# Routing table of a mixture-of-experts kernel: indirect scatters to DRAM replaced by one-hot products

## Chip, cores and metric

The kernel runs on one core of a Trainium2 chip. The metric is the device time of the core in microseconds (us). The kernel before was timed in three runs: 739.37 us in the median, 734.49 to 740.71.

## The reference, cut to what matters

Two blocks follow each other. The first is attention over 8 batches, 8 heads, 576 positions and a head width of 64, half of the heads with a local mask of 32 positions, half with a strided one. Its output, 512 columns for each of the 4608 positions, is the input x of the second block, a mixture of 8 experts. Each position goes to exactly one expert, and which one depends on the positions ahead of it in its batch:

```
for s in range(S):
    fresh_e = int(np.argmax(logits[b, s]))
    if s == 0 or local_gate[b, s] < 0.5:
        e = fresh_e
    else:
        e = prev_e if prev_e >= 0 else fresh_e
    prev_e = e
    ...
    h = np.maximum(x[b, s] @ w1[e], 0.0)
    out[b, s] = p[e] * (h @ w2[e])
```

w1[e] is 512 x 1024 and w2[e] is 1024 x 512; p is the softmax of the logits. All is fp32.

## The kernel before

**Attention.** The loop of attention() (L414-L445) goes over 32 steps n, one for each of 8 batches and 4 pairs of heads, and three more to drain. It is a software pipeline written out by hand: at step n the scores of n (L252, exp on ScalarE at L256, mask on VectorE at L263), the values of n-1 (L276, norm at L289-L290), the transposes of n-2 (L317), the gate logits of a batch (L336) and its gates (L354-L379). Stores of x to DRAM (L301, L307) and all loads go out from SyncE's queue. Other work is hung on steps by two lists: `also[n]`, and `steps`, the 16 VectorE sums and differences of the first expert's weights that a Strassen-like product needs (L703: first four tiles ws1-ws4 of w1, two ops each, then wt1-wt4 of w2). Two of these are issued at each step from n=9 on.

**Routing** is done in two rounds of four batches. Router.steps (L511-L570) gives for each position a slot (idx) and a gate value (p): transposes (L523), scans on VectorE (L529, L536), products for the counts (L541, L542) and back (L556). A slot says place within the 128 rows of a tile (lane), tile and expert. Round 0 hangs on steps 19 to 23 of attention, round 1 on the first pair of the experts' part.

**The table** tells which token and gate value stands in which slot, 128 lanes x 56 columns (NT). It lies in DRAM (slots). It is filled with "no token" at the start (L503-L505). Each round then scatters its (token, gate) pairs to it with 20 indirect DMAs of GpSimd (L577), one for each of 5 chunks of 128 positions and 4 batches, each with up to 128 entries of 8 bytes. At the end it is read back once (fetch, L643) and turned to gather indices (table, L647). Round 0's scatters hang on steps m=24 to 33, two a step, and share GpSimd's queue with the gathers of x (L737). Since the experts start before round 1 is done, the first four tiles (columns of experts 0 and 1, two tiles each) are also made on chip from round 0 alone (early, L585-L639): for each of 20 groups of positions a one-hot matrix of lanes (L620) and a matrix `put` of 20 columns, a one-hot of 4 columns times five bf16 values (L615), are multiplied on TensorE and summed over the 20 groups (L627). The five values are exact parts: the token number as 64 a + b, the gate as three bf16 pieces.

**Experts.** Each expert gets its weights by SyncE's queue into one of two buffers W[0], W[1]. Two tiles of 128 rows make a pair: pair_hidden (seven products L807, VectorE adds L795, ScalarE copies L814 and relus L794) and pair_output (L843, L854-L857), with gather (L737), scale (L743), transposes (L750), row sums (L759) and a scatter of the result (L763) around them. A list of places is run at fixed points in between: four in pair_hidden, four in pair_output; it holds the round's steps, the weight sums of the next expert and the scatters (L1002-L1020). The first pair is expert 0's, the second, `other`, expert 1's, the third, `second`, again expert 0's, with rows of round 1. A count of tiles per expert then picks an arm of a switch (L975); arms() (L649) makes it.

[...] GpSimd's queue holds scatters, gathers and, later, output scatters one behind the other.

Of the kernel before, what the change touches and what calls it, by code (L numbers as in the profile page):

```python
# [93 lines left out]
@with_exitstack  # L94
def attention_then_scomoe(ctx: ExitStack, tc: tile.TileContext, qkl, qks, vl, vs, wg, q, k, vl2, vs2, wg2, w1, w2, out):
    nc = tc.nc
    dram = ctx.enter_context(tc.tile_pool(name="dram", bufs=1, space=DRAM))
    xd = dram.tile([N, D], F32, name="xd")
    keep = ctx.enter_context(tc.tile_pool(name="keep", bufs=1))
    ident = keep.tile([P, P], F32, name="ident")  # L100
    make_identity(nc, ident)

    with ExitStack() as fast:
        once = fast.enter_context(tc.tile_pool(name="once", bufs=1))
        router = Router(once, dram, tc, ident)
        one = Weights(once)
        spot = (once.tile([P, 2, D], F32, name="x0"), once.tile([P, 2, DK, P], F32, name="xt"),
                once.tile([P, 4, 2, P], F32, name="tt"))
        with tc.manual_schedule():
            moe = Experts(nc, tc, xd, w1, w2, out, ident, router, one, spot)  # L110
            with ExitStack() as part:
                attention(part, tc, qkl, qks, vl, vs, wg, xd, ident, router, moe)
            with ExitStack() as part:
                moe.run(part)
        flag = router.flag


    redo = nc.values_load(flag, min_val=0, max_val=P + N,
                          skip_runtime_bounds_check_because="a count of at most 128 rows and of pairs")
    with tc.If(redo > 0):  # L120
        with ExitStack() as slow:
            general(slow, tc, q, k, vl2, vs2, wg2, w1, w2, xd, out, ident)
# [20 lines left out]
def attention(ctx, tc, qkl, qks, vl, vs, wg, xd, ident, router, moe):  # L143
# [260 lines left out]
    also[n] += [lambda: early.extend(router.early(bank, moe.spot)), lambda: early.pop(0)()]  # L404
    for n in range(m + 1, m + 6):
        also[n].append(lambda: early.pop(0)())
    for i, do in enumerate(router.scatters(0)):
        also[m + i // 2].append(do)
# [5 lines left out]
    for n in range(len(units) + 3):  # L414
# [20 lines left out]
        for do in steps[:2] if n >= 9 else []:  # L435
            do()
            steps.remove(do)
# [10 lines left out]
class Router:  # L448


    def __init__(self, pool, dram, tc, ident):
# [6 lines left out]
        self.tok = f("tok", [P, CH, B, 2], I32)  # L458
# [9 lines left out]
        self.io, self.jc = f("io", [P, P], BF16), f("jc", [P, 2, EARLY])  # L468
        self.vals = f("vals", [P, CH, RB, 5], BF16)
        self.put = f("put", [P, CH * RB, 5, 2 * EARLY], BF16)  # L470
        self.pool = pool
        self.T = dram.tile([P * NT, 2], I32, name="slots")

    def constants(self):
# [19 lines left out]
        ids = pool.tile([P, CH, B], I32, name="ids")  # L494
        nc.gpsimd.iota(ids, pattern=[[P, CH], [S, B]], base=0, channel_multiplier=1)
        nc.vector.tensor_copy(self.tok[:, :, :, 0], ids)
        for name, pattern, mult, o in (("io", [[1, P]], 0, self.io), ("jc", [[E, 2], [1, EARLY]], 0, self.jc),
                                       ("v0", [[P // 64, CH], [S // 64, RB]], 0, self.vals[:, :, :, 0]),
                                       ("v1", [[0, CH], [0, RB]], 1, self.vals[:, :, :, 1])):
            t = pool.tile(list(o.shape), I32, name=f"i{name}")  # L500
            nc.gpsimd.iota(t, pattern=pattern, base=1 if name == "v0" else 0, channel_multiplier=mult)
            nc.vector.tensor_copy(o, t)
        nc.gpsimd.iota(self.tab[:, :, 0], pattern=[[0, NT]], base=SKIP, channel_multiplier=0)  # L503
        nc.gpsimd.iota(self.tab[:, :, 1], pattern=[[0, NT]], base=0, channel_multiplier=0)
        nc.gpsimd.dma_start(out=self.rows(0, XT, E), in_=self.tab.rearrange("p (k e) v -> p k e v", e=E))  # L505

    def rows(self, k0, k1, e):

        return self.T.rearrange("(k p e) v -> p k e v", p=P, e=E)[:, k0:k1, 0:e]

    def steps(self, r, bank):  # L511
# [39 lines left out]
        def back():  # L551
# [16 lines left out]
            nc.vector.tensor_copy(self.tok.bitcast(F32)[:, :, bs, 1], p)  # L568
# [3 lines left out]
    def scatters(self, r):  # L572
        def one(t, b):
            m = min(P, S - t * P)

            def do():
                s = self.nc.gpsimd.indirect_dma_start(  # L577
                    out=self.T, out_offset=bass.IndirectOffsetOnAxis(ap=self.idx[0:m, t, b:b + 1], axis=0),
                    in_=self.tok[0:m, t, r * RB + b], in_offset=None, bounds_check=P * NT - 1, oob_is_err=False)
                self.tc.declare_no_dep(s.ins, group="slots", reason="scatters write different slots")  # L580
                self.tc.add_to_no_dep_group("slots", s.ins)
            return do
        return [one(t, b) for b in range(RB) for t in range(CH)]

    def early(self, bank, spot):  # L585
# [4 lines left out]
        lo, hi, code, lof = f("elo", [P, n], I32), f("ehi", [P, n], I32), f("ecode", [P, n]), f("elof", [P, n])  # L590
        at, rest, got = f("at", [P, n, 2 * EARLY], BF16), f("rest", [P, CH, RB]), f("got", [P, 5, 2 * EARLY])
        num, skip, gs = f("num", [P, 2 * EARLY]), f("skip", [P, 2 * EARLY]), f("gs", [P, 2 * EARLY])
        idx, val = flat(self.idx), self.vals.rearrange("p t b v -> p (t b) v")

        room = (spot[1].rearrange("p a k x -> p (a k x)").bitcast(BF16), spot[2].rearrange("p i a x -> p (i a x)").bitcast(BF16))
        lane = lambda i: room[2 * i // n][:, i % (n // 2) * P:(i % (n // 2) + 1) * P]

        def where():
# [6 lines left out]
            nc.vector.tensor_tensor(at, across(self.jc.rearrange("p k e -> p (k e)"), [P, n, 2 * EARLY]),  # L605
                                    spread(code, [P, n, 2 * EARLY]), op=Alu.is_equal)

        def what():
            v = [self.vals[:, :, :, i] for i in range(5)]
            nc.vector.tensor_copy(v[2], self.p)  # L610
            nc.vector.tensor_tensor(rest, self.p, v[2], op=Alu.subtract)
            nc.vector.tensor_copy(v[3], rest)
            nc.vector.tensor_tensor(v[4], rest, v[3], op=Alu.subtract)
            for i in range(5):
                nc.vector.tensor_tensor(self.put[:, :, i], at, spread(val[:, :, i], [P, n, 2 * EARLY]), op=Alu.mult)  # L615

        def lanes(a, b):
            def do():
                for i in range(a, b):
                    nc.vector.tensor_scalar(lane(i), self.io, lof[:, i:i + 1], None, Alu.is_equal)  # L620
            return do

        def products():
            o = bank()[:, 0:10 * EARLY].rearrange("p (v j) -> p v j", v=5)
            for i in range(n):
                m = min(P, S - i // RB * P)
                nc.tensor.matmul(o, lhsT=lane(i)[0:m], rhs=self.put[0:m, i], start=(i == 0), stop=(i == n - 1))  # L627
            nc.vector.tensor_copy(got, o)

        def numbers():  # L630
            tab = self.tab1.rearrange("p k e v -> p (k e) v")
            nc.vector.scalar_tensor_tensor(num, got[:, 0], 64.0, got[:, 1], Alu.mult, Alu.add)
            nc.vector.tensor_tensor(gs, got[:, 2], got[:, 3], op=Alu.add)
            nc.vector.tensor_scalar(skip, num, 0.0, SKIP + 64.0, Alu.is_equal, Alu.mult)
            nc.vector.tensor_scalar(self.gi1.rearrange("p k e -> p (k e)"), num, -64.0, 0.0, Alu.add, Alu.max)
            nc.vector.tensor_tensor(tab.bitcast(F32)[:, :, 1], gs, got[:, 4], op=Alu.add)
            nc.vector.scalar_tensor_tensor(tab[:, :, 0], num, -64.0, skip, Alu.add, Alu.add)

        return [where, what, lanes(0, n // 2), lanes(n // 2, n), products, numbers]  # L639

    def fetch(self):

        self.nc.gpsimd.dma_start(out=self.tab.rearrange("p (k e) v -> p k e v", e=E), in_=self.rows(0, XT, E))  # L643

    def table(self):

        self.nc.vector.tensor_scalar(self.gi, self.tab[:, :, 0], N - 1.0, None, Alu.min)  # L647
# [79 lines left out]
class Experts:  # L727
# [41 lines left out]
    def run(self, ctx):  # L769
# [234 lines left out]
        self.gather(other)  # L1004
        todo = router.steps(1, bank)
        places = slots(todo, [2, 2, 1, 1]) + slots(sums, [2, 2, 2, 1, 1])
        more = router.scatters(1)
        for place, n in zip(places[4:], (4, 2, 2, 2, 2)):
            place += [more.pop(0) for _ in range(n)]
        output(self.first, W[0], pair_hidden(self.first, W[0], places), other, places)  # L1010
        second = rows(0, 1, (2, 3))
        places = slots(sums, [2, 2, 2, 2])
        for place in places:
            place += [more.pop(0) for _ in range(2)]
        arms = router.arms(bank)
        places[3].append(lambda: next(arms))
        places += [[lambda: next(arms), router.table, lambda: self.gather(second)]]
        h = pair_hidden(other, W[1], places)
        router.fetch()
# [484 lines left out]
```

## Time and profile before

| | before |
|---|---|
| median of 3 runs | 739.37 us |
| time of the profiled execution | 738.92 us |
| its span, first to last instruction | 737.2 us |
| granted TensorE clock, mean | 0.959 |
| TensorE matmul busy | 683.0 us, 93% |
| VectorE busy | 353.4 us, 48% |
| ScalarE busy | 195.5 us, 27% |
| GpSimd busy | 134.7 us, 18% |
| scatters of slots L577 | 40, 40.9 us of GpSimd |
| gathers of x L737 | 40, 40.4 us of GpSimd |
| scatters of results L763 | 40, 45.5 us of GpSimd |
| early table's products L627 | 20, 173 ns each in the trace with latency |
| attention, about | 0 to 199.6 us |
| experts | 199.6 us to the end |

PE is TensorE's matmul, PEld its weight load, DVE VectorE, ACT ScalarE, POOL GpSimd. The page cuts the span in 40 slices of 18.43 us; a digit is the busy share of a slice in tenths, and PEclk is the clock that TensorE was granted, in tenths. In a row of groups come line, engine, operation, output and inputs, count, busy time, mean of one, the idle time just before, and what ended it. In the timeline a row has start, length, engine, line, operation, count, and in brackets the idle time before it with what ended it: "issue" is a wait for nothing that the profile shows, "remote" a wait for an event of which it has no record.

### The profile page before, as it was taken

The page shows a single profiled execution, that of the slowest core. Times are in us where ns is not written, and L with a number is a line of the kernel's source. Part 1 is how long each engine was busy: PE and PEld are TensorE (multiplying, and loading weights), DVE is VectorE, ACT ScalarE, POOL GpSimd, SP SyncE. Part 2 cuts the span into 40 slices and gives each one's busy share as a digit, 9 for nine tenths or more (in the row PEclk, how much of TensorE's full clock was granted, in tenths as well). Part 3 has the DMA queues.
Part 4 walks back from the last instruction along what each step waited for, and adds up shares of the span by engine and source line. Part 5 has one row for each costly group of instructions (what it writes and reads, how often), then busy time and mean ns, then how long its engine had stood idle before and what let it go on. Part 6 is the DMA issues. An engine that isn't in the chain of part 4 may idle for free.

```text
span 737.2 us, 14832 instructions
## 1 busy us (share of the span) xinstructions
PE 683.0 (93%) x6034; PEld 586.5 (80%) x6034; DVE 353.4 (48%) x843; ACT 195.5 (27%) x357; POOL 134.7 (18%) x150
## 2 busy tenths in 40 slices
PE   7999999497899699999999999999999999999992
PEld 5878887385698589985998899999589899789961
DVE  6568766272466534451463265455126646524300
ACT  2544443141321122212222123122322222222210
POOL 3000001405127330221121120221012012111010
PEclk9999999597699899999999999999999999999997
DMA  9797887731360022615321711720171262010010
GB/s 325 275 328 267 279 286 256 249 84 52 95 228 30 3 86 67 238 38 173 109 74 47 254 47 50 251 73 21 39 257 59 76 210 66 32 37 30 18 50 13
DMA packets 37803, 95.33 MB, mean 129 GB/s; under 512 B 5230, under 2 KB 14446, under 8 KB 37632
## 3 DMA queue, kind: packets, MB, share of 16 engines
q1 hardware_dynamic: 29616, 73.77, 29.0%
q0 software_dynamic: 7488, 19.56, 8.4%
q8 instruction: 66, 1.08, 0.6%
q14 instruction: 105, 0.86, 0.4%
q10 hardware_dynamic: 528, 0.07, 0.1%
HBM read 74.41 MB, written 19.49 MB: 127 GB/s over the span
## 4 chain that ended last, share of the span: by engine, by line
PE 79%; issue 7%; DVE 5%; DMA 3%; another core or an unknown queue 3%; ACT 1%; POOL 1%; SPq 0%; DVEq 0%; POOLq 0%; ACTq 0%
PE mps L843 26%; PE lps L807 25%; PE vps L276 5%; PE sps L252 4%; PE tps L317 3%; PE lps L898 3%; PE mps L909 3%; PE xps L750 2%; DMA w1t<-in_w_dram 2%; PE mps L935 2%; PE lps L919 1%; PE sps L246 1%; PE tps L336 1%; PE vps L354 1%
## 5 line engine op out<-in xcount | busy, mean ns | idle before, releaser
L763 POOL DMA_INDIRECT out_dram<-y,tab x40 | 45.5, 1138 | 323.9 <-DVE y L795 217.4
L807 PE MATMUL lps<-tt,ws 128*128 128x128 f32 x768 | 91.5, 275 | 0.4 <-issue 0.2
L807 PEld LDWEIGHTS lps<-tt,ws 128*128 128x128 f32 x768 | 88.5, 192 | 0.8 <-DVE u L795 0.4
L843 PE MATMUL mps<-wt,k 128*128 128x256 f32 x384 | 85.6, 379 | 0.0
L843 PEld LDWEIGHTS mps<-wt,k 128*128 128x128 f32 x384 | 72.9, 190 | 9.9
L577 POOL DMA_INDIRECT slots<-tok,idx x40 | 40.9, 1023 | 147.5 <-DVE tok L568 135.9
L807 PE MATMUL lps<-xt,w1t 128*128 128x128 f32 x512 | 64.8, 281 | 2.6 <-ACT y L941 1.4
L807 PEld LDWEIGHTS lps<-xt,w1t 128*128 128x128 f32 x512 | 62.1, 196 | 6.1 <-ACT y L941 2.8
L795 DVE TENSOR_TENSOR h<-lps,u 128x512 f32<-128x512 f32 x48 | 33.2, 691 | 66.5 <-PE lps L807 57.3
L843 PE MATMUL mps<-w2t,h 128*128 128x256 f32 x256 | 61.3, 383 | 0.0
L737 POOL DMA_INDIRECT x<-xd,gi x40 | 40.4, 1009 | 112.5 <-PE lps L807 34.9
L252 PE MATMUL sps<-qk 64*128 64x96 f32 (+2 forms) x704 | 55.4, 288 | 4.9 <-issue 4.1
L252 PEld LDWEIGHTS sps<-qk 64*128 64x128 f32 (+2 forms) x704 | 45.5, 188 | 14.8 <-issue 12.5
L256 ACT ACTIVATE e<-sps 128x576 f32<-128x576 f32 (+1 forms) x64 | 41.2, 651 | 58.4 <-PE sps L252 40.8
L843 PEld LDWEIGHTS mps<-w2t,h 128*128 128x128 f32 x256 | 48.1, 193 | 6.0
L794 ACT ACTIVATE h<-h 128x512 f32<-128x512 f32 x48 | 30.3, 630 | 75.5 <-DVE h L795 71.7
L794 ACT ACTIVATE h<-lps 128x512 f32<-128x512 f32 x28 | 16.5, 594 | 86.8 <-PE lps L807 58.8
L795 DVE TENSOR_TENSOR u<-lps,p 128x512 f32<-128x512 f32 x16 | 11.1, 692 | 57.9 <-PE lps L807 32.3
L807 PE MATMUL lps<-xt,ws 128*128 128x128 f32 x256 | 33.1, 285 | 6.0 <-DVE h L795 6.0
L743 ACT ACTIVATE x<-x,tab 128x512 f32<-128x512 f32 (+1 forms) x40 | 27.2, 718 | 40.6 <-DMA x<-xd,gi 26.9
L807 PEld LDWEIGHTS lps<-xt,ws 128*128 128x128 f32 x256 | 31.5, 201 | 6.2 <-DVE h L795 6.2
L276 PE MATMUL vps<-vl,e 128*64 128x65 f32 x768 | 29.4, 235 | 7.0 <-issue 4.7
(222 smaller groups left out, 977.4 us busy)
## 6 DMA issues: line engine op xcount, KB each, us to landing
w1t<-in_w_dram SPq DMA_DIRECT2D x8, 2048.0 KB
w2t<-in_w_dram SPq DMA_DIRECT2D x8, 2048.0 KB
qk<-in_qkl_dram SPq DMA_DIRECT2D x16, 592.0 KB
qk<-in_qks_dram SPq DMA_DIRECT2D x16, 576.0 KB
vl<-in_vf_dram SPq DMA_DIRECT2D x8, 780.0 KB
vs<-in_vg_dram SPq DMA_DIRECT2D x8, 639.8 KB
xd<-xl SPq DMA_DIRECT2D x16, 288.0 KB
xd<-xs SPq DMA_DIRECT2D x64, 63.0 KB
```

The lines of the kernel that those rows point to most:

```text
L252: nc.tensor.matmul(ps[0:m, h, c:c + w], lhsT=t[r, S + j * width:S + j * width + m], rhs=t[r, j * width:j * width + w], start=(u.local and ...
L256: nc.scalar.activation(e[0:kb, :, 0:n], ps[0:kb, :, 0:n], Act.Exp, bias=0.0, scale=1.0 / DH ** 0.5)
L276: nc.tensor.matmul(ps[a * HALF:(a + 1) * HALF, h, i], lhsT=u.e[0:m, h, q0:q0 + HALF], rhs=vt[0:m, j, 2 * i2 + h], start=(i == 0 and h == 0 ...
L317: nc.tensor.transpose(ps[:, t], src[:, t], ident)
L577: s = self.nc.gpsimd.indirect_dma_start(out=self.T, out_offset=bass.IndirectOffsetOnAxis(ap=self.idx[0:m, t, b:b + 1], axis=0), in_=self.t ...
L737: self.nc.gpsimd.indirect_dma_start(out=r.x[0:r.m, i], out_offset=None, in_=self.xd[0:r.rows], in_offset=bass.IndirectOffsetOnAxis(ap=r.gi ...
L743: self.nc.scalar.activation(r.x[0:r.m, i], r.x[0:r.m, i], Act.Copy, scale=r.gate[i][0:r.m])
L763: s = self.nc.gpsimd.indirect_dma_start(out=self.out, out_offset=bass.IndirectOffsetOnAxis(ap=r.si[i][0:r.m], axis=0), in_=y[0:r.m, i], in ...
L794: relu = lambda o, i: nc.scalar.activation(o, i, Act.Relu)
L795: add = lambda o, i, p: nc.vector.tensor_tensor(o, p, i, op=Alu.add)
L807: nc.tensor.matmul(ps[:, f], lhsT=m[:, kk, f * P:(f + 1) * P], rhs=v[:, kk], start=(start and f == 0 and kk == 0), stop=(kk == 1), skip_gr ...
L843: nc.tensor.matmul(ps[:, 0:256], lhsT=m[:, f], rhs=v[:, f], start=(start and f == 0), stop=(f == 3), skip_group_check=True)
```

## The change

Both rounds make the whole table of 56 columns by products, as `early` did for four. Gone are the DRAM tile, its fill and read-back (fetch, table), the 40 scatters, and the copies of token numbers and gates that they read. The new function is Router.table(r, bank, w, big), with the same six parts as early, called for both rounds:

- `where`: parts of the slot, and `at`, the one-hot of 56 columns for 20 groups (1120 elements).
- `what`: the bf16 parts on VectorE, and `put` (20 groups x 5 values x 56 columns) by 15 multiplies of 392 or 336 elements, now on GpSimd.
- `some`, twice: the one-hots of lanes, 4 groups in one VectorE op of 512 elements, bf16.
- `products`: 20 products of 280 columns; round 1 adds what round 0 left in `got`.
- `numbers`: in round 0 for the four early columns, in round 1 for all 56.

Scratch is borrowed: `put` and `at` lie in the four wt tiles of W[0] (round 0) and W[1] (round 1), the lanes in xt (round 0) and in the result buffer y0 (round 1). So wt sums may be written only once the round's products have read it. W[0]'s sums are issued from n=13 (ws) and from n=m+5=29 (wt) instead of from n=9. In round 1 the parts are hung on places 3 to 6 of the first pair; products come at place 0 of the second pair, ahead of its third product, with 3, 3 and 2 wt sums at places 1, 2 and 3 where there were 2 at each of four, and numbers and the gather of `second` at place 2, where the gather had been in the pair's output part.

```diff
-    also[n] += [lambda: early.extend(router.early(bank, moe.spot)), lambda: early.pop(0)()]
+    lanes = moe.spot[1].rearrange("p a k x -> p (a k x)")
+    also[n] += [lambda: early.extend(router.table(0, bank, moe.W[0], lanes)), lambda: early.pop(0)()]
     for n in range(m + 1, m + 6):
         also[n].append(lambda: early.pop(0)())
-    for i, do in enumerate(router.scatters(0)):
-        also[m + i // 2].append(do)
...
-        for do in steps[:2] if n >= 9 else []:
+        for do in steps[:2] if n >= (13 if len(steps) > 8 else m + 5) else []:
...
-            nc.vector.tensor_tensor(at, across(self.jc.rearrange("p k e -> p (k e)"), [P, n, 2 * EARLY]),
-                                    spread(code, [P, n, 2 * EARLY]), op=Alu.is_equal)
+            nc.vector.tensor_tensor(at, across(self.jc, [P, n, NT]), spread(code, [P, n, NT]), op=Alu.is_equal)
...
-            for i in range(5):
-                nc.vector.tensor_tensor(self.put[:, :, i], at, spread(val[:, :, i], [P, n, 2 * EARLY]), op=Alu.mult)
+            for a in range(0, n, per):
+                m = min(n, a + per) - a
+                o = room[a // per][:, 0:m * wide].rearrange("p (i v j) -> p i v j", v=5, j=NT)
+                for i in range(5):
+                    nc.gpsimd.tensor_tensor(o[:, :, i], at[:, a:a + m], spread(val[:, a:a + m, i], [P, m, NT]), op=Alu.mult)
...
-                for i in range(a, b):
-                    nc.vector.tensor_scalar(lane(i), self.io, lof[:, i:i + 1], None, Alu.is_equal)
+                for c in range(a, b, 4):
+                    l0, _, t = lanes[c >= nb]
+                    nc.vector.tensor_tensor(t[:, c - l0:c - l0 + 4], across(self.io, [P, 4, P]),
+                                            spread(lof[:, c:c + 4], [P, 4, P]), op=Alu.is_equal)
...
-            o = bank()[:, 0:10 * EARLY].rearrange("p (v j) -> p v j", v=5)
+            o = bank()[:, 0:wide]
             for i in range(n):
                 m = min(P, S - i // RB * P)
-                nc.tensor.matmul(o, lhsT=lane(i)[0:m], rhs=self.put[0:m, i], start=(i == 0), stop=(i == n - 1))
-            nc.vector.tensor_copy(got, o)
+                nc.tensor.matmul(o, lhsT=lane(i)[0:m], rhs=put(i)[0:m], start=(i == 0), stop=(i == n - 1))
+            o = o.rearrange("p (v j) -> p v j", v=5)
+            if r:
+                nc.vector.tensor_tensor(got, o, got, op=Alu.add)
+            else:
+                nc.vector.tensor_copy(got, o)
...
         places = slots(todo, [2, 2, 1, 1]) + slots(sums, [2, 2, 2, 1, 1])
-        more = router.scatters(1)
-        for place, n in zip(places[4:], (4, 2, 2, 2, 2)):
-            place += [more.pop(0) for _ in range(n)]
+        todo = []
+        places[3] += [lambda: todo.extend(router.table(1, bank, W[1], other_y)), lambda: todo.pop(0)()]
+        for place in places[4:7]:
+            place.append(lambda: todo.pop(0)())
         output(self.first, W[0], pair_hidden(self.first, W[0], places), other, places)
         second = rows(0, 1, (2, 3))
-        places = slots(sums, [2, 2, 2, 2])
-        for place in places:
-            place += [more.pop(0) for _ in range(2)]
+        places = [[lambda: todo.pop(0)()]] + slots(sums, [3, 3, 2])
+        places[2] += [lambda: todo.pop(0)(), lambda: self.gather(second)]
         arms = router.arms(bank)
         places[3].append(lambda: next(arms))
-        places += [[lambda: next(arms), router.table, lambda: self.gather(second)]]
+        places += [[lambda: next(arms)]]
         h = pair_hidden(other, W[1], places)
-        router.fetch()
```

In the changed kernel the multiplies stand at L604, the lanes at L610, the products at L618.

## The prediction

> **What bounds the kernel now.** I read the page's slices first (PE busy, granted clock), then the timeline around each dip, then the DMA queues and the busy time in the same stretches.
>
> The page's slices of 18.4 us, PE above PEclk, show a kernel held by TensorE almost everywhere, with dips at 129-147, 166-203 and 240-258 us. Group L577 is the 40 scatters of slots (count, then busy us, mean ns, idle).
>
> ```profile
> PE   7999999497899699999999999999999999999992
> ...
> PEclk9999999597699899999999999999999999999997
> ...
> L577 POOL DMA_INDIRECT slots<-tok,idx x40 | 40.9, 1023 | 147.5 <-DVE tok L568 135.9
> ```
>
> The timeline of the first dip (start, us, engine, what, count, idle before it and releaser):
>
> ```profile
> 124.89 1.04 POOL L577 DMA_INDIRECT slots<-tok,idx  x1 [110.88 <-DVE tok L568]
> ...
> 130.65 0.31 PEld L252 LDWEIGHTS sps<-qk 64*128 64x128 f32 x3 [1.01 <-issue]
> ...
> 135.20 0.20 DVE L289 RECIPROCAL sums<-vps 128x6 f32<-128x6 f32 x1 [7.56 <-remote]
> ...
> 138.92 0.97 POOL L577 DMA_INDIRECT slots<-tok,idx  x1 [0.30 <-issue]
> ...
> 142.55 1.19 ACT L256 ACTIVATE e<-sps 128x576 f32<-128x576 f32 x2 [16.38 <-remote]
> ```
>
> Twelve scatters go out back to back from 124.9 to 139.9. PE, VectorE and ScalarE then stop together, waiting for nothing that the profile names ("issue", "remote"), and resume at 142.4. The second dip has eight scatters (172.1 to 181.9, all resume at 183 to 184), the third the last ten of round 1 (to 246.7, resume at 248.3):
>
> ```profile
> 242.66 0.60 ACT L794 ACTIVATE h<-lps 128x512 f32<-128x512 f32 x1 [10.69 <-remote]
> ...
> 248.08 0.98 POOL L643 DMA_DIRECT2D tab<-slots  x1 [1.40 <-DMA slots<-tok,idx]
> 248.30 0.69 DVE L795 TENSOR_TENSOR h<-lps,u 128x512 f32<-128x512 f32 x1 [8.13 <-remote]
> ```
>
> The DMA queues of 216-250 us [...] one packet of the two instruction queues (q8, q14) in 34 us, beside 815 of POOL's (columns: packets, MB, share of 16 engines). Over the program q8 has 66 packets, one per 11 us, and q14 105.
>
> ```profile
> q0 software_dynamic: 815, 0.60, 6.6%
> q8 instruction: 1, 0.02, 0.3%
> ```
>
> The DMA engines are hardly busy there, so it isn't bandwidth; [...]
>
> [...]
>
> **Removed.** (A) The gate products L354 of successive batches start at 76.27 and 95.02, a period of 18.75. Those around the first burst start at 114.69 and 152.44: 37.75. Of the excess of 19.0, 1.4 is the round's own L556 and L541 work, which stays: 17.6 lost, 12.7 standing still (14.8 us for 2.1 us of products) and the rest in the low clock after it. (B) Scores at 175.3 should take 2.5 us and end at 184.2: 6.4. L354 before them was 2.2 late, and 184.2 to 199.6 runs at clock 0.72, about 3.4 of 15.4: 12.0. (C) The second pair lasts 229.34 to 268.72, 39.4; a normal one 344.74 to 370.62, 25.9. Less 0.5 for L669-L672: 13.0, late gather of second included. Sum 42.6. The 41 us of POOL issue, fetch L643, fill L505, copies L568 and L647 go too, off the path.
>
> **Added, round 0.** PE: L627 takes 0.87 us for 20 products of 20 columns. The new have 280; L246's pairs of 252 and 324 columns (0.43, 0.49 us) give 0.42 ns a column, so 117 ns each, 2.3 us: +1.5. VectorE: the table of places grows from 80 to 1120 elements (233 ns for 80, 1 ns an element more: 1.3), the copy of results by 0.3, five put ops (0.23 each) leave, and 5 lane ops of 512 at 0.68 replace twenty in 3.4: about zero. POOL: 15 multiplies, 5600 elements, [...] In the trace that work may begin at 149.75 and the products come at 161.44, 11.7 later, [...] The wt sums move from n=13-16 to n=29-32: 8 x 0.68 us of VectorE in the drain, covered by its idle (half of 150-200 us); uncovered 5.4, I take 1. The ws sums start four steps later, when weights have landed: nothing. Sum 8.3.
>
> **Added, round 1.** Before trace's times, since its third stall starts only at 236.4. VectorE gets 0.9 + 1.3 for places before h12, so sums, bf16 parts (1.0) and v2 move from 223.5 to about 224.4. [...] Lanes (1.4, then 2.0) stand ahead of v3 and v4, so the row sum that the second product of the pair waits for moves from 229.0 to 233.4. That product ended at 233.1 and now ends at 235.4 [...] The products add 2.4, a lower clock after the wait 1: 11.6. Behind POOL's multiplies stand two output scatters, whose tile is needed a pair later, and the gather of second, which the numbers release two products of the pair later, near 252; it was needed at 264 (ScalarE's scale), so it is early even so.
>
> Against the profiled execution: span 737.2 - 42.6 + 8.3 + 11.6 = 714.5. Its time is 738.92, 1.7 above its span, so 716.2; the median is 0.45 above that execution: 717. [...]
>
> **Rivals.**
> Fast multiplies: GpSimd runs them at the pace of its 128x576 memset (584 ns, 1.0 ns an element), 5.7 us a round, and all waits for it vanish. Remaining adds 1.5 + 1 and 2.3 + 2.4: 704. [...]
>
> Slow multiplies, which ends slower: GpSimd becomes the bound at the table's products, PE standing in both rounds. With the adds above at 19.9, nothing is gained when each round's multiplies take 11.3 us more, [...] Only the lack of a row speaks for it.
>
> The change doesn't do what removing scatters suggests: [...] Then 717 + 42.6 = 760, rounded. Against: 60-110 us has ten packets of the instruction queues and no such stall beside 264 GB/s of loads.
>
> Loads bind: with A gone attention runs ahead of its DMA. From 127.6 to 171 some 6.8 MB moved; at 265 GB/s that is 25.6 us for 26.4 of PE work, barely hidden. If stores hold tiles back by a third of A, 723.
>
> **How the numbers follow.** Forecast 0.63, own range 706 to 725; fast multiplies 0.15; loads 0.08; slow multiplies 0.09; stalls stay 0.05. A measurement of this kernel can tell about 1% from no change, 732 to 747. Faster: 0.63 + 0.15 + 0.06 of loads + 0.03 of slow multiplies = 0.87. Within: 0.02 + 0.03 = 0.05. Slower: 0.03 + 0.05 = 0.08. The range goes down past the fast case, 702, and up to 731, leaving about 0.05 below and 0.13 above.
>
> **What would show it.** The stretches 124-143, 171-184 and 236-250 lose "remote" idle on VectorE and ScalarE, and PEclk stays at 9 or more but for short dips; the instruction queue keeps its pace. PE waits for POOL at L618, by about 4 us in round 0 and 3 at its arrival in round 1; [...] The second pair lasts about 38 us (39.4 - 13.0 + 11.6). It would be wrong if "remote" idle stays without L577, [...]

## The result and the profile after

The changed kernel takes 732.14 us in the median of 16 runs (729.11 to 737.96), the kernel before 737.24 of 16 (732.62 to 741.38): ratio 0.9935, interval 0.9912 to 0.9958. So it is faster, but by 0.65%; the forecast was 717, the stated range 702 to 731, and 732.14 lies just inside the 732 to 747 that the prediction counts as no change. Medians here are those of all executions; ratios leave out executions over 1.5% above the fastest of their kernel. The profiled execution took 730.94 us, with a span of 729.2 us at clock 0.968.

The page's slices of the changed kernel, now 18.23 us each, with the group of the multiplies (count, busy us, mean ns, idle before and its releaser):

```profile
PE   8999999898978899999999999999999999999980
...
PEclk9999999987999999999999999999999999999995
...
L604 POOL TENSOR_TENSOR wt<-wt,vals 128x392 bf16<-128x392 bf16 (+1 forms) x30 | 30.1, 1036 | 150.9 <-DVE wt L590 116.6
```

TensorE's slice of 4 at 129-147 us and its 6 at 240-258 us are gone. What is left of the dips lies mostly at 164-255 us, the lowest a 7 at 201-219, and the last slice has fallen from 2 to 0. The time by stretch, in us (a pair is counted from its first product; in the middle what the prediction's own terms give):

| stretch | before | predicted | after |
|---|---|---|---|
| start to the first product of the first pair | 199.5 | 178.2 | 180.3 |
| first pair | 29.8 | 29.8 | 34.4 |
| second pair | 39.4 | 38.0 | 38.6 |
| third pair to the start of the last result scatter | 457.4 | 457.4 | 458.0 |
| from there to the end of the span (called the tail below) | 11.0 | 11.0 | 17.9 |
| sum, before rounding | 737.2 | 714.5 | 729.2 |

The miss of 14.7 us is 2.0 in attention, 5.2 in the two pairs, 0.6 behind them and 6.9 at the very end, where nothing of the change runs. The timeline of GpSimd's last instruction, first the kernel before, then the changed one, has no later busy record on any engine:

```profile
726.16 0.91 POOL L763 DMA_INDIRECT out_dram<-y,tab  x1 [8.59 <-ACT y L941]
```

```profile
711.26 0.93 POOL L756 DMA_INDIRECT out_dram<-y,tab  x1 [8.57 <-ACT y L934]
```

At that point the changed kernel is 14.9 us ahead; at the end of the span, 8.0.

The timeline of TensorE around the end of the first pair, first in the kernel before (start, length, then the idle time before and its releaser):

```profile
227.61 1.89 PE L843 MATMUL mps<-w2t,k 128*128 128x256 f32 x8
229.34 1.95 PE L807 MATMUL lps<-xt,w1t 128*128 128x128 f32 x16
231.13 3.74 PE L807 MATMUL lps<-tt,ws 128*128 128x128 f32 x32
```

The same products and the rest of the two pairs in the changed kernel:

```profile
202.30 3.62 PE L836 MATMUL mps<-wt,k 128*128 128x256 f32 x16
206.12 1.99 PE L836 MATMUL mps<-wt,k 128*128 128x256 f32 x8 [0.20 <-DVE v L788]
207.95 1.04 PE L743 MATMUL xps<-ident,x 128*128 128x128 f32 x8
211.10 3.68 PE L836 MATMUL mps<-w2t,k 128*128 128x256 f32 x8 [2.12 <-DVE v L788]
214.62 1.95 PE L800 MATMUL lps<-xt,w1t 128*128 128x128 f32 x16
220.72 3.16 PE L800 MATMUL lps<-tt,ws 128*128 128x128 f32 x16 [4.15 <-DVE tt L752]
223.67 2.65 PE L618 MATMUL xps<-wt,y 128*128 128x280 bf16 x16
...
241.46 3.37 PE L836 MATMUL mps<-w2t,h 128*128 128x256 f32 x8 [1.97 <-ACT q L852]
```

Three waits, 2.12, 4.15 and 1.97 us. None is for GpSimd: the table's products at 223.67 follow at once. Each wait is followed by products in a low clock, 0.50 to 0.51 for 3.4 us each time (from 211.2, 221.4 and 241.9): eight L836 products take 3.68 and 3.37 us where they took 1.99 at 206.12. VectorE's timeline says what was late, first two rows of the kernel before, then the changed one:

```profile
223.88 1.28 DVE L703 TENSOR_TENSOR ws<-ws,w1t 128x512 f32<-128x512 f32 x2
225.21 0.42 DVE L795 TENSOR_TENSOR v<-mps,v 128x256 f32<-128x256 f32 x1
```


```profile
205.98 2.23 DVE L696 TENSOR_TENSOR ws<-ws,w1t 128x512 f32<-128x512 f32 x2
208.13 2.59 DVE L610 TENSOR_TENSOR y<-io,elof 128x512 bf16<-128x512 bf16 x2
210.64 0.41 DVE L788 TENSOR_TENSOR v<-mps,v 128x256 f32<-128x256 f32 x1
...
211.43 2.61 DVE L696 TENSOR_TENSOR ws<-w1t 128x512 f32<-128x512 f32 x2
213.96 2.50 DVE L610 TENSOR_TENSOR y<-io,elof 128x512 bf16<-128x512 bf16 x2
216.37 1.24 DVE L610 TENSOR_TENSOR wt<-io,elof 128x512 bf16<-128x512 bf16 x1
...
218.80 0.97 DVE L752 TENSOR_TENSOR tt<-xt 128x256 f32<-128x256 f32 x1
```

The add at 210.64, which in the kernel before follows the weight sums at once, stands behind two lanes (L610), and the row sum at 218.80 behind three more. A pair of weight sums L696 takes 1.28 us elsewhere, here 2.23 and 2.61. Beside them GpSimd's multiplies run, from 203.91 to 220.38:

```profile
128.76 2.61 POOL L604 TENSOR_TENSOR wt<-wt,vals 128x392 bf16<-128x392 bf16 x2 [116.57 <-DVE wt L590]
133.42 11.15 POOL L604 TENSOR_TENSOR wt<-wt,vals 128x392 bf16<-128x392 bf16 x13 [2.04 <-DVE vals L596]
...
203.91 16.47 POOL L604 TENSOR_TENSOR wt<-wt,vals 128x392 bf16<-128x392 bf16 x15 [32.18 <-issue]
```

One of the prediction's signs, the single packet of the instruction queues, turned out to be worth nothing. In the changed kernel's stretch of 216 to 250 us the instruction queue q8 has two packets where the kernel before had one, and no engine has "remote" idle, there or elsewhere in its trace. The row of q8 in that stretch (packets, MB, share of 16 engines):

```profile
q8 instruction: 2, 0.03, 0.5%
```

### The profile page after: what moved, and what is told of

It is laid out like the page before. It is cut to its first block, busy times and chain, and to the rows that moved or that the text cites. A ratio compares the mean times of both kernels' runs of the same rounds, so it can differ in the third digit from the quotient of the medians.

```text
span 729.2 us, 14800 instructions
## 1 busy us (share of the span) xinstructions
PE 681.1 (93%) x6054; PEld 584.4 (80%) x6054; DVE 371.4 (51%) x842; ACT 195.5 (27%) x357; POOL 122.8 (17%) x135
## 4 chain that ended last, share of the span: by engine, by line
PE 81%; DVE 9%; issue 5%; ACT 1%; POOL 1%; DMA 0%; another core or an unknown queue 0%; ACTq 0%; DVEq 0%; POOLq 0%; SPq 0%
PE lps L800 26%; PE mps L836 24%; PE vps L276 5%; PE sps L252 5%; PE tps L317 3%; PE lps L891 3%; PE mps L902 3%; PE xps L743 2%; PE mps L928 2%; PE lps L912 1%; PE sps L246 1%; PE vps L354 1%; PE tps L336 1%; DVE ws L696 1%; DVE y L610 1%
## 5 line engine op out<-in xcount | busy, mean ns | idle before, releaser
L836 PE MATMUL mps<-wt,k 128*128 128x256 f32 x384 | 85.9, 380 | 0.2 <-DVE v L788 0.2
L836 PEld LDWEIGHTS mps<-wt,k 128*128 128x128 f32 x384 | 72.8, 190 | 10.5 <-DVE v L788 0.6
L836 PE MATMUL mps<-w2t,h 128*128 128x256 f32 x256 | 62.0, 386 | 2.0 <-ACT q L852 2.0
L604 POOL TENSOR_TENSOR wt<-wt,vals 128x392 bf16<-128x392 bf16 (+1 forms) x30 | 30.1, 1036 | 150.9 <-DVE wt L590 116.6
L836 PEld LDWEIGHTS mps<-w2t,h 128*128 128x128 f32 x256 | 48.1, 193 | 8.4 <-ACT q L852 2.4
L252 PE MATMUL sps<-qk 64*128 64x96 f32 (+2 forms) x704 | 51.9, 286 | 0.1
L252 PEld LDWEIGHTS sps<-qk 64*128 64x128 f32 (+2 forms) x704 | 43.6, 188 | 8.3 <-issue 7.3
L787 ACT ACTIVATE h<-h 128x512 f32<-128x512 f32 x48 | 30.3, 630 | 73.6 <-DVE h L788 69.8
L787 ACT ACTIVATE h<-lps 128x512 f32<-128x512 f32 x28 | 16.5, 594 | 92.8 <-PE lps L800 73.2
L744 ACT COPY xt<-xps 128x512 f32<-128x512 f32 (+1 forms) x38 | 19.9, 566 | 54.1 <-PE xps L743 54.0
L836 PE MATMUL mps<-w2t,k 128*128 128x256 f32 x128 | 32.2, 397 | 2.1 <-DVE v L788 2.1
L921 DVE COPY h<-lps 128x512 f32<-128x512 f32 x4 | 2.8, 692 | 56.2 <-PE lps L920 56.2
```

The costliest lines, as they stand in the source:

```text
L252: nc.tensor.matmul(ps[0:m, h, c:c + w], lhsT=t[r, S + j * width:S + j * width + m], rhs=t[r, j * width:j * width + w], start=(u.local and ...
L604: nc.gpsimd.tensor_tensor(o[:, :, i], at[:, a:a + m], spread(val[:, a:a + m, i], [P, m, NT]), op=Alu.mult)
L787: relu = lambda o, i: nc.scalar.activation(o, i, Act.Relu)
L836: nc.tensor.matmul(ps[:, 0:256], lhsT=m[:, f], rhs=v[:, f], start=(start and f == 0), stop=(f == 3), skip_group_check=True)
```

## The experiments

**Does the fallback hold what was given back?** The program ends with a branch to a long fallback that these inputs don't take. Two kernels leave out the flag, the branch and the fallback, and so the answer for inputs that need it; everything else is as it was.

```diff
-    redo = nc.values_load(flag, min_val=0, max_val=P + N,
-                          skip_runtime_bounds_check_because="a count of at most 128 rows and of pairs")
-    with tc.If(redo > 0):
-        with ExitStack() as slow:
-            general(slow, tc, q, k, vl2, vs2, wg2, w1, w2, xd, out, ident)
```

The kernel before without it:

> The kernel before without its fallback (the load of the flag, the branch and the general code, which this input doesn't run; it leaves out the answer for inputs that need it). Theory T1, a part of the gain is given back after the last scatter of results, where the engines load the flag and jump over the fallback: this loses the 10.1 us that lie between the last scatter and the end, all but some 4, so about 731 (6 under before). Theory T2, that tail is noise of one execution: the same here, since both say only that the tail shrinks.

The changed kernel without it:

> The changed kernel without the same fallback. T1: its tail of 17.0 us shrinks to the same 4 or so, so it lies 13 to 15 us under b_noif, about 717. T2, the tail is noise and the work itself gained no more than the 5 us of the medians: 5 to 8 under b_noif, about 725.

Measured: 732.85 us (ratio to the kernel before 0.9943, 0.992 to 0.9966) and 725.81 us (0.9813, 0.9761 to 0.9865). The two differ by 7.0 us in the medians and 9.6 by the ratios, where theory T1 asks for 13 to 15 and T2 for 5 to 8; with the fallback it is 5.1 and 4.8. So the fallback holds at most 2 to 5 us of what was given back. The tail is 6.3 us without the fallback in the kernel before, and 12.0 in the changed one: 5.7 us longer there too, where it was 6.9. The branch and the fallback are not its cause.

**Are the scatters the cause of the stalls?** The changed kernel with the 40 scatters put back at their old places, into a DRAM tile that nothing reads.

```diff
+    for i, do in enumerate(router.scatters(0)):
+        also[m + i // 2].append(do)
...
+        more = router.scatters(1)
+        for place, n in zip(places[4:], (4, 2, 2, 2, 2)):
+            place += [more.pop(0) for _ in range(n)]
...
+        for place in places:
+            place += [more.pop(0) for _ in range(2)]
```

> The changed kernel with the 40 scatters of slots put back at their old places, to a DRAM tile that nobody reads, nothing else. Theory S, [...] the stalls come back, remote idle of VectorE and ScalarE in three bursts, 25 to 40 us slower than the changed kernel, 757 to 772. Rival R, the stalls came from something else that the change removed (the fill, the read-back and its waits): within 5 us of the changed kernel, 732 to 737.

Measured: 767.38 us, ratio 1.0411 (1.0359 to 1.0463), 35 us above the changed kernel. Between the two profiled executions, 36.4 us apart, 19.9 lie in attention, 14.4 in the second pair and 4.8 in the tail, with 3.1 less in the first pair. The page's slices have dips again, and the timeline the "remote" idle:

```profile
PE   7999999877886599999999999999999999999960
...
L569 POOL DMA_INDIRECT slots<-tok,idx x40 | 40.5, 1014 | 124.3 <-DVE tok L560 112.8
```

```profile
263.41 0.60 ACT L806 ACTIVATE h<-lps 128x512 f32<-128x512 f32 x1 [29.36 <-remote]
```

So the scatters cause the stalls, some 30 us without the tail. By what means they do so was not shown; the packet count (two where there was one) doesn't tell it.

**Round 1's lanes later.** The lanes move from places 5 and 6 of the first pair to 7 and 8, and products, weight sums and numbers move back behind them.

```diff
-        for place in places[4:7]:
-            place.append(lambda: todo.pop(0)())
+        for i in (4, 7, 8):
+            places[i].append(lambda: todo.pop(0)())
...
-        places = [[lambda: todo.pop(0)()]] + slots(sums, [3, 3, 2])
+        places = [[], [lambda: todo.pop(0)()]] + slots(sums, [4, 4])
```

> The changed kernel with round 1's lane ops moved from the first pair's output places 1 and 2 to 3 and 4, its products from place 0 to 1 of the second pair, wt sums 4 and 4 at places 2 and 3, numbers, gather and arms one place later. Theory D, VectorE's order [...] cost the 4.6 us by which the first pair grew and the 4.2 us for which the second pair's second product waits: both go, 5 to 8 us faster than the changed kernel, about 725. Rival W, GpSimd's multiplies themselves set the pace: no gain, 731 to 734.

Measured: 728.36 us, ratio 0.9896 (0.9863 to 0.9929), 3.8 us under the changed kernel, or 2.9 by the ratios: more than rival W's nothing, less than theory D's 5 to 8, as one of the two waits stayed. TensorE's timeline has the first pair from 181.81 to 212.09, 30.3 us, without the wait of 2.12:

```profile
210.36 1.89 PE L836 MATMUL mps<-w2t,k 128*128 128x256 f32 x8
212.09 1.95 PE L800 MATMUL lps<-xt,w1t 128*128 128x128 f32 x16
218.68 3.62 PE L800 MATMUL lps<-tt,ws 128*128 128x128 f32 x18 [4.65 <-DVE tt L752]
```

The row sums still stand behind two lanes and the wait for them stays, so the second pair takes 38.2.

**Multiplies on VectorE.** The same 30 multiplies with nc.vector in place of nc.gpsimd, five with the first values and five ahead of each half of the lanes.

```diff
-                    nc.gpsimd.tensor_tensor(o[:, :, i], at[:, a:a + m], spread(val[:, a:a + m, i], [P, m, NT]), op=Alu.mult)
+                nc.vector.tensor_tensor(o[:, :, i], at[:, a:a + m], spread(val[:, a:a + m, i], [P, m, NT]), op=Alu.mult)
```

> The changed kernel with its 30 multiplies on VectorE instead of GpSimd, in three groups of five per round (with the first values, and ahead of each half of the lanes). From the row of the comparison of codes (1.32 us for 1120 elements) a 392-element multiply should be about 0.47 us there, so 7 us per round more on VectorE, and no GpSimd arithmetic beside it. Theory X (what the first pair lost, 34.3 us against 29.7, is VectorE slowed [...] while GpSimd multiplies): VectorE's weight sums and lanes are back at 1.28 to 1.4 us for two, the fourth output product doesn't wait 2.1 us, first pair 30 to 32 us, time 727 to 730 if the stretch after the last result scatter stays at 17.9 us. Theory W (VectorE has simply too much to do there): first pair as long or longer, 732 to 737. Theory G (the longer stretch after the last result scatter, 17.9 against 11.0 us, comes with GpSimd arithmetic in the program): that stretch is back at 11 us, and the time is another 6 to 7 us lower, 720 to 724. Theory L (it depends on where GpSimd's code happens to lie): it takes some other value, not to be foretold.

Measured: 733.05 us, ratio 0.9962 (0.9937 to 0.9987). VectorE's timeline of this kernel shows two sums or two lanes in 1.28 us again, and five multiplies ahead of the lanes:

```profile
206.81 1.28 DVE L699 TENSOR_TENSOR ws<-ws,w1t 128x512 f32<-128x512 f32 x2
208.01 2.47 DVE L606 TENSOR_TENSOR wt<-wt,vals 128x392 bf16<-128x392 bf16 x5
210.39 1.28 DVE L613 TENSOR_TENSOR y<-io,elof 128x512 bf16<-128x512 bf16 x2
211.60 0.42 DVE L791 TENSOR_TENSOR v<-mps,v 128x256 f32<-128x256 f32 x1
```

The add still waits for the same two lanes, 30.1 us into the first pair where it was 30.4; TensorE waits 2.25 us for it. The first pair takes 32.4 us instead of 34.4, the second 40.0 instead of 38.6. A multiply takes 0.49 us on VectorE and some 0.86 on GpSimd (11.15 for 13), and the two placements cost about the same, with theory X's 727 to 730 not reached. The tail stayed at 17.2 us, so it doesn't come with GpSimd arithmetic.

**The tail: GpSimd's arithmetic or where its code lies?** 59 and 29 memsets of one element a partition at the start of GpSimd's stream, and, in the kernel before, one memset and one multiply there.

```diff
+        idle = pool.tile([P, 1], F32, name="idle")
+        for _ in range(59):
+            nc.gpsimd.memset(idle, 0.0)
```

> The changed kernel with 59 memsets of one element each put into GpSimd's stream at the start, where GpSimd is idle for some 100 us, so that its stream in the part that runs has as many instructions as that of the kernel before. Theory L ([...] that depends on where GpSimd's code lies): the stretch moves from 17.9 us by more than 2 us, perhaps to 11, and the time moves with it (725 to 727 for 11 us). Theory G (it comes with GpSimd arithmetic): 17 to 18.5 us, time 732.

> The same with 29 memsets. Theory L: a stretch after the last result scatter that differs from 17.9 us or from that with 59 memsets by more than 2 us. Theory G: 17 to 18.5 us in both, time 732.

```diff
+        idle = pool.tile([P, 2 * P], BF16, name="idle")
+        nc.gpsimd.memset(idle, 0.0)
+        nc.gpsimd.tensor_tensor(idle[:, P:], idle[:, 0:P], idle[:, 0:P], op=Alu.mult)
```

> The kernel before with one memset and one bf16 multiply (128x128, of a tile that nothing reads) put into GpSimd's stream at the start. Theory G (any GpSimd arithmetic in the program lengthens the stretch after the last result scatter): 17 to 18 us instead of 11.0, and a time about 6.5 us above that of the kernel before, 743 to 744. Theory L: near 11 us, or a jump by several us that has nothing to do with the multiply; the likeliest is no change, 737.

Measured: 730.90, 731.78 and 735.36 us (ratios 0.9927, 0.9948 and 1.0018), with tails of 18.0, 17.1 and 10.5. Both theories fall. The answer was in the trace's records of instructions that count as neither busy nor waiting. Behind its last result scatter GpSimd has a DRAIN: from 734.40 to 736.35 us in the kernel before, from 721.77 to 728.38 in the changed one. In the changed one no other engine has a record between 722.52 us and 728.56, when all four wait for a semaphore that GpSimd raised at 728.52, just behind the drain. Ahead of the drain, and beside the last result scatter, stands an INC_SWDGE_SEM of GpSimd ("increment" here), whose length varies as well (0.46 to 2.23 us in the kernel before once 56 DMAs had been issued). From the trace's records of each kernel, in us:

| kernel | tail | drain behind the last result scatter | last increment | DMAs issued by GpSimd |
|---|---|---|---|---|
| before | 11.0 | 1.95 | 0.64 | 122 |
| changed | 17.9 | 6.61 | 1.76 | 80 |
| changed, multiplies on VectorE | 17.2 | 6.61 | 1.77 | 80 |
| changed, scatters put back | 22.7 | 9.88 | 2.56 | 120 |

The increment beside the last result scatter is 0.63 us in the kernel before and 1.78 in the changed one. With the last increment and the last drain that makes 6.9 us, all by which the tail grew.

From 80 to 120 DMAs the drain grows by 3.27 us, 0.082 each, and 6.61 / 80 is 0.083. The kernel before doesn't fit: 122 DMAs and a drain of 1.95 us. Its increments grow from 1.31 us (56 DMAs issued) to 2.23 (102), and then fall to 0.46 (111). At 0.082 us each its drain would be that of 24 DMAs, near the 11 to 20 issued since that fall. What makes the increments fall isn't shown. The number of DMAs alone doesn't decide it: with the scatters put back, 120 had been issued and the last increment was 2.56 us.

**A drain per expert.** GpSimd is told to drain where it has little to do.

```diff
             if nxt is not None:
                 self.gather(nxt)
+                nc.gpsimd.drain()
```

> The changed kernel with an explicit drain of GpSimd after the gather of the next expert's rows, once per expert for the first seven of them, where GpSimd then has nothing to do for 5 to 12 us. In the trace GpSimd's last drain takes 6.61 us (80 indirect DMAs issued by then) against 1.95 us in the kernel before (122 DMAs), and 9.88 us with the 40 scatters put back (120 DMAs); its increments of DMA semaphores grow by 0.02 us with each DMA issued, and in the kernel before they fall from 2.23 to 0.46 us between the 102nd and the 111th DMA. Theory R ([...]): the seven drains take about 0.8 us each, hidden, the last one about 1.3 us for the 14 to 18 DMAs since, the last increments about 0.5 us instead of 1.77, the stretch after the last result scatter 10 to 11 us instead of 17.9, time 724 to 726. Theory N (a drain costs what it costs with the count of all DMAs so far [...]): drains that grow from 1 to 5.5 us, stretch 17.9 us as it was, time 732 or above.

> The changed kernel with a drain of GpSimd per expert, where it was so far only measured on the chip on which the kernel before took 703 us (719.7 us there). Theory R: 724 us where the kernel before takes 736 and the changed one 732, as it takes away 7 to 8 us of the stretch after the last result scatter, so that the drains hold somewhat more than half of the best version's 13.5 us over the changed kernel. Theory N: no gain, 731 to 733, and the best version's gain comes from the order alone.

On a chip where the kernel before takes 737.64 it measured 722.37 us, ratio 0.9815 (0.9764 to 0.9865), and 9 to 10 us less than the changed kernel. The tail is 9.3 us, the drain in it 1.20 for the 16 DMAs since the drain before it, the last increment 0.44: theory R holds in what it says of the tail. The seven drains took 4.9 to 6.2 us each and not 0.8; they come just behind two gathers, and why they took so long isn't shown. GpSimd's idle time covers most of them: the stretch from the third pair to the last result scatter is 459.8 us, where the changed kernel had 458.0.

**Both halves of the lanes behind the row sums, alone and with the drains.**

```diff
-        for place in places[4:7]:
-            place.append(lambda: todo.pop(0)())
+        places[4].append(lambda: todo.pop(0)())
...
-        places = [[lambda: todo.pop(0)()]] + slots(sums, [3, 3, 2])
+        places = [[lambda: todo.pop(0)(), lambda: todo.pop(0)()], [lambda: todo.pop(0)()]] + slots(sums, [4, 4])
```

> As the kernel with round 1's lanes later, but with both halves of the lanes behind the row sums of the second pair, in the first place of the second pair (there one half stood ahead of the row sums and the second pair's products waited 4.65 us for them). Theory D (what is lost in the two pairs is VectorE's order: the output's sums and the row sums stand behind lanes): the wait for row sums falls from 4.65 to 2 to 3 us, second pair 35 to 36 us instead of 38.2, time 725 to 727. Theory E ([...]): the wait stays above 4 us, time 728.

> Both edits together. Theories R and D: gains add up, 6 to 7 us by the drains and 6 by the order, 718 to 721, ratio to the kernel before 0.975 to 0.980. If R falls, 726; if D falls, 721 to 722.

> The changed kernel with round 1's lanes behind the row sums of the second pair and a drain of GpSimd per expert, 710.9 us on the chip of the last runs. Theory C: 710 to 716 here too, so the best of the four where the kernel before takes 736 (ratio 0.965 to 0.973), and about 1% slower than it where that takes 703.

Where the kernel before takes 737.01 us, both edits together take 718.05: ratio 0.9756 (0.9688 to 0.9825), the best of all. TensorE's timeline of that run has pairs of 30.3 us (181.91 to 212.19) and 35.8 us (212.19 to 248.00), and the wait for row sums has halved, as theory D had it (with the same order and no drains it is 2.32 too, and the tail stays at 18.1):

```profile
212.19 1.95 PE L800 MATMUL lps<-xt,w1t 128*128 128x128 f32 x16
216.46 5.42 PE L800 MATMUL lps<-tt,ws 128*128 128x128 f32 x32 [2.33 <-DVE tt L752]
...
223.50 2.07 PE L618 MATMUL xps<-wt,y 128*128 128x280 bf16 x16
225.50 0.65 PE L618 MATMUL xps<-wt,wt 64*128 64x280 bf16 x4
...
248.00 1.95 PE L800 MATMUL lps<-xt,w1t 128*128 128x128 f32 x16
```

**A chip on which the kernel before is fast.** Three of these runs fell on one chip where the kernel before took 703.18 us (699.16 to 708.8) instead of 736 to 738. There the kernel with drains took 719.68, ratio 1.023 (1.0161 to 1.0298), that with both halves of the lanes behind the row sums 718.53, 1.0211 (1.0119 to 1.0303), and that with both edits 710.92, 1.0119 (1.0042 to 1.0196). All three are slower than the kernel before on that chip. The unchanged kernels were then run again on other chips:

> The kernel before, unchanged, for its profile beside the others of this call: on the chip of the last three runs it took 703.2 us, on those of all earlier runs 736 to 737. Theory C (the stalls of its scatters of slots differ by chip, everything else is alike): where it takes 736, its profile has the three stalls and first pair at about 200 us; where it takes 703, the bursts of scatters are there and the stalls A, B and C (17.6, 12.0 and 13.0 us by the prediction's count) are mostly gone, 34 us together, first pair at about 182 us. Theory K (that chip is faster altogether): the stalls are there, and all other stretches are shorter in proportion, 4.5%.

> The changed kernel, unchanged, on the same chip. It has no scatters of slots. Theory C: 727 to 732 us on any chip, so faster than before by 0.7% where that takes 736, and slower by 3.5 to 4% where that takes 703. Theory K: 732 where the kernel before takes 736, 699 where that takes 703.

> The changed kernel with the 40 scatters of slots put back to a table that nothing reads, 767.4 us and 35 us above the changed kernel where the kernel before took 736. Theory C: 765 to 769 us where the kernel before takes 736; where that takes 703, within 5 us of the changed kernel, but for some 3 us of the last drain. Theory K: 35 us above the changed kernel everywhere.

> The kernel before, unchanged, for its profile on one more chip. Where it takes 736: the three stalls are in it, first pair near 200 us. Where it takes about 703, as on one chip so far, theory C says that the bursts of scatters are there and the stalls of PE beside them are not, first pair at about 182 us or less, and theory K that all stretches are shorter alike.

None of these runs fell on that chip. The kernel before took 736.62 and 736.86 us, the changed one 731.53 (0.9944, 0.9918 to 0.9969), and that with the scatters put back 766.14 (1.0418, 1.0346 to 1.049), as on the first chips. On the odd chip the kernel with both edits was 7.1 us faster than elsewhere and the one with drains 2.7, but the kernel before 33 to 35. The kernel with both edits, at 718.05, also missed theory C's 710 to 716. Its profiled executions differ by 8.4 us between the two chips, and 6.1 of these lie in attention (first pair at 175.78 and 181.91). A chip that is faster altogether (theory K) would not gain 33 us on one kernel and 3 to 7 on the others; that the scatters stall little there would. No profile of the kernel before was taken on that chip, nor was the changed kernel run there, so this stays open.

## Why the prediction went wrong

**Removed, A, B and C (42.6 us): A held where the kernel before takes 737; B and C show only together with what was added.** "Remote" idle left with the scatters. The gate products around the first burst start 20.9 us apart, where A leaves 37.75 - 17.6 = 20.15:

```profile
115.01 1.25 PE L354 MATMUL vps<-fold,lT 128*128 128x9 f32 x12 [0.65 <-DVE sums L289]
...
135.93 1.25 PE L354 MATMUL vps<-fold,lT 128*128 128x9 f32 x12 [0.28 <-DVE sums L289]
```

The next two batches take 43.1 us together where they took 45.9, so 2.8 less against the 3.7 that B and the adds of round 0 give. Attention as a whole ended 19.3 us earlier against 21.3. The scatters put back cost 19.9 us in attention, where A and B are 29.6, and 14.4 in the second pair, where C is 13.0; but some of their bursts then stand behind the multiplies, so this doesn't measure the same terms. The low clock behind the stall that A counts was 0.69 (142.4 to 152.0 us in the kernel before). By what means the scatters held the other engines up isn't shown.

**Added, round 0 (8.3): the sum was near, its terms not.** Of the 8.3 us, 4.3 for a wait for GpSimd's multiplies and 1.5 for VectorE beside them were the author's estimates, which nothing in the profile of the kernel before showed; the ends of the author's own range, 706 and 725, rest on such estimates too. The batch that holds the table's products, 135.93 to 161.71, is 7.0 us longer than the normal 18.75. GpSimd's multiplies were done at 144.57, ahead of the products at 147.69, so the wait of 4.3 for GpSimd didn't come. In its place stood VectorE work that was slower while GpSimd multiplied: two lanes took 2.44 us (1.28 for the next two, behind the multiplies), small gate ops up to 0.81 instead of 0.2, and TensorE waited 1.67 for a norm behind them; the products took 3.50 us, not 2.3, at clock 0.71. The table of places took 1.33 us for its 1120 elements, against 1.3: the 1 ns an element is the pace of VectorE's fp32 ops in the kernel before (420 ns for 256 elements, L759, and 683 for 512, L703).

**Added, round 1 (11.6): the second pair came out at 38.6 us against 38.0, in part by luck, and the first pair was missed.** That the row sum would stand behind the lanes was foreseen, with a product ending at least 2.3 us late; TensorE waited 4.15. That the table's products would start 8.2 us late, behind GpSimd's multiplies, was the author's estimate, which the profile of the kernel before didn't show. The wait for GpSimd was 0, as the multiplies ended at 220.38 and TensorE came at 223.67; that a lower clock (0.51 from 221.4 and 0.50 from 241.9, for 3.4 us each) and the wait of 1.97 for ScalarE filled its place is the luck. (ScalarE's copy stands behind a relu that needs the add at 239.79, and that add stands behind the small ops of arms() on VectorE, L648 to L658, from 237.41; in the kernels with later lanes, where these ops also come a place later, that wait is gone.) The step that failed is "Lanes (1.4, then 2.0) stand ahead of v3 and v4": it was followed only to the row sum. But TensorE's last output product of the first pair waits for the add v3 itself, 2.12 us, and then runs 1.8 us longer at clock 0.50: most of the 4.6 us by which the first pair grew, costed at nothing. With the lanes moved behind v3 and v4, the wait is gone and the first pair back at 30.3; this gave 3.8 us. Both halves moved behind the row sums too gave 4.3 on top of the drains (722.37 to 718.05, on two chips).

A multiply took some 0.86 us in round 0 (11.15 for 13) and 1.10 beside VectorE's weight sums and lanes in round 1 (16.47 for 15), or 2.3 and 2.9 ns an element; what the sum took for it had no row of the kernel before behind it. In round 1 two VectorE ops that take 1.28 us elsewhere took 2.23 to 2.61 beside the multiplies. What this slowing costs can't be told from the run with the multiplies on VectorE: there two ops take 1.28 us again, but five multiplies of 2.47 us stand ahead of the add, about as much as the slowing took.

**Not in the sum at all: the end of the program, 6.9 us.** It is the largest part of the miss, and the second step that failed: "Against the profiled execution: span 737.2 - 42.6 + 8.3 + 11.6" leaves the stretch after the last result scatter as it was, without a reason. In the kernel before GpSimd's increments fell from 2.23 to 0.46 us between the 102nd and the 111th of 122 DMAs; in the changed one, with 80, they grew from 0.50 (14 DMAs issued) to 1.78 (79) without a fall, and the last two with the drain took 6.9 us longer at the end. Why they fell in the one is not known; with the scatters put back the last was 2.56. The drains per expert show that the drain and the increments are what the tail grew by: with them the drain at the end is 1.20 us, the last increment 0.44 and the tail 9.3.

**Rivals.** Fast multiplies fall by the measured 13.8 and 16.5 us a round, where that rival took 5.7. Slow multiplies fall as TensorE waited for GpSimd at the table's products in neither round. That stalls stay falls by "remote" idle, of which none is left. Loads didn't bind: from 100 to 181 us waits for a DMA sum to 0.4 us in the changed kernel. The forecast was right in sign, and the two parts together left 8.0 us of the 22.7 that the sum gave (737.2 to 714.5).

## What to carry to other kernels

When work moves off one queue, ask on each engine that takes it what stands behind the new instructions in program order, and follow each of these to the engine that waits: here the place of five VectorE ops was worth about 4 us, and the engine of the 30 multiplies next to nothing. The end of a program belongs to the sum: look at what the engines do after the last busy record, also where no instruction there changes. And time a change on more than one chip before trusting a gain of a few per cent.

## What was not expected of the hardware

GpSimd's drain behind the last result scatter took 6.61 us with 80 DMAs issued and 9.88 with 120, some 0.08 us for each; with drains in the middle it took 1.20 us, with 16 issued since the last of these. The kernel before, with 1.95 us and 122 issued, doesn't follow this. On one chip of several the kernel before took 703 us instead of 737, while kernels without the 40 scatters changed by 3 to 7 us.
